# Gated linear attention feeding an expert layer: attention stages placed anew between the matrix products, with a drain of TensorE between groups of outputs

## The chip, the cores and the metric

One core of a Trainium2 chip runs the whole program. The metric is the device time of one execution in microseconds (us), as the median of the runs. TensorE (PE in the profile) multiplies matrices and is fed weights by a second row of the profile (PEld); VectorE (DVE), ScalarE (ACT) and GpSimd (POOL) do the rest, and SyncE (SP) issues nearly all transfers (DMAs).

## What is computed

Two layers follow each other. The first is attention with a decaying state, for 4 batches and 8 heads of width 48, over 768 positions; its output, 3072 tokens of 384 numbers, goes through a wide layer of 2048 units with a piecewise quadratic activation:

```python
f = 1 / (1 + exp(-f_logit))
for t in range(768):
    state = f[t] * state + outer(k[t], v[t])
    y[t] = q[t] @ state
x = y.reshape(3072, 384)
h = x @ w_in
g = where(h >= 1, h, where(h <= -1, 0, (h + 1) ** 2 / 4))
out = g @ w_out
```

## The kernel before, in words

**Tiles.** The 768 positions are cut into 6 tiles of 128 (index i). With 4 batches a tile is 512 tokens. The expert layer works tile by tile, in 16 *units* of 128 hidden columns each, so there are 96 units, numbered u = 16 i + j. `unit_1(u)` multiplies the tile with its piece of w_in (9 matrix products of 128x128 by 128x512 on line 265, 3 row blocks times 3 terms, since each fp32 number is split into a high and a low part), and then ACT and DVE form the activation: `act_1` and `act_2` on ACT (lines 268 and 271), `act_3` on DVE (line 276), the high part on ACT (line 884) and the low part on DVE (line 279). `unit_2(u)` multiplies that with the piece of w_out (9 products on line 286). TensorE gets them in the order unit_1(u), then what attention has at u, then unit_2(u-1).

**Weights.** Each of the 32 weight pieces comes in as 64-bit floats, and is turned into a high and a low part before the first tile's units need it: ACT line 362, DVE line 364, a cast on ACT or DVE (line 367), DVE line 368. This happens once, during units 0 to 15.

**Attention.** Heads are taken in pairs; n counts pairs of heads, 4 to a tile (n = 4 i + p), and stages work on n and n+1 together. The *gates* of a tile (function `gate`, 3 per tile) are an exponential and a logarithm on ACT, a running sum on DVE (line 498), two more exponentials, and two products on DVE that scale the keys and queries in place (lines 503 and 504). The fourth pair's rows are spread over the three tiles' spare rows and are gathered by small transfers (`move`, line 295). TensorE's part of attention has four stages:

- *turns*: transposes the keys (line 635; from the third tile on DVE does it, line 650);
- *scores*: keys times queries, 64 small products (line 616), masked by DVE (line 622);
- *parts*: keys times values, 64 small products (line 754), summed into the state by DVE (lines 775 and 777); *states* is its simpler form for the first tile (line 733);
- *outputs*: 32 products that mask one diagonal half (called `begin`, line 683), 64 products with the state (line 705, called `before`), and 32 products for the other half (line 683 again), all added up in two PSUM banks; ACT and DVE then round the result (lines 655 and 656) and small transfers (line 295) put it in place for the expert layer.

**Order.** The order on TensorE is written out: tables `TURNS` and `VISITS` say for each pair n at which unit each of its stages stands, and `AFTER` does so for the first tile. A stretch of small attention products stands between two runs of large ones. `begin` runs in the same stretch as `parts`, one unit or more before the rest of `outputs`. The order on ACT, DVE, SP and POOL comes from a list scheduler, `Plan.order`: each operation has a cost from the table `COST`, transfers land `LANDING` + `PER_KB` per KB after their issue, and of what is ready the one that is due first goes first. What comes out is a fixed order in which each engine waits for its operands. Where the planner sees TensorE idle for over 500 ns, it puts in filler products (function `warm`, line 331).

```python
TURNS = {4: 4, 5: 5, 6: 9, 7: 9, 8: 19, ...}
VISITS = {4: (5, 6, 7), 6: (10, 12, 13), 8: (21, 22, 25), 10: (25, 26, 28), ...}
AFTER = {0: (("turn", 0), ("turn", 1)), 1: (("states", 0),), 2: (("turn", 2), ("turn", 3)), 3: (("states", 2),)}
```

In `VISITS` the three numbers of a pair are the units of its scores, of its `begin` with `parts`, and of its outputs. Where two pairs name one unit, both stages stand in one stretch; that is so at seven units already (25, 28, 37, 40, 47, 61 and 70: outputs of one pair, then scores of the next).

Of the kernel before, what the change touches and what calls it, by code (L numbers as in the profile page):

```python
# [23 lines left out]
C = 128  # L24
# [24 lines left out]
SMALL_PRODUCTS = ("gates", "scores", "heads", "own", "tile", "both", "begin", "before", "part", "states", "parts", "half", "turn")  # L49

HOP, LANDING, PER_KB, NEAR, ADDING, PATIENCE, FLAG_BY = 200, 2200, 3.0, 3500, 1500, 0, 60000
COST = dict(gates=870, log=500, mm=227, scores=1100, heads=950, own=1200, tile=680, both=1090, begin=480, before=930, part=560, states=850, parts=830, turn=350, first=110, last=95,
            rows=316, scan=1140, dve=602, small=200, half=490, sums=467, gate=600, act=575, bits=520, join=465, part_hi=440, cast_384=330, cast=400, round=485, copy=520, turned=412, sig=538, decay=226,
# [3 lines left out]
TURNS = {4: 4, 5: 5, 6: 9, 7: 9, 8: 19, 9: 19, 10: 25, 11: 25, 12: 28, 13: 28, 14: 37, 15: 37, 16: 40, 17: 40, 18: 47, 19: 47, 20: 61, 21: 61, 22: 70, 23: 70}  # L57
VISITS = {4: (5, 6, 7), 6: (10, 12, 13), 8: (21, 22, 25), 10: (25, 26, 28), 12: (28, 32, 37), 14: (37, 39, 40), 16: (40, 46, 47), 18: (47, 60, 61), 20: (61, 69, 70), 22: (70, 75, 77)}
# [3 lines left out]
AFTER = {0: (("turn", 0), ("turn", 1)), 1: (("states", 0),), 2: (("turn", 2), ("turn", 3)), 3: (("states", 2),)}  # L62
# [11 lines left out]
class Plan:  # L74
# [40 lines left out]
    def order(self):  # L115
        index = {o: n for n, o in enumerate(self.ops)}
        for o in reversed(self.ops):
            tail = o.cost + (LANDING + PER_KB * o.kb + (ADDING if o.engine == "POOL" else 0) if o.kb else o.near)
            o.late = min((u.late - (HOP if u.engine != o.engine or len(o.choices) + len(u.choices) > 2 else 0) for u in o.users), default=0) - tail - o.late_by
# [13 lines left out]
        while done < len(self.ops):  # L133
# [33 lines left out]
            if o.kb:  # L167
                wire = max(wire, end) + PER_KB * o.kb
                end = wire + LANDING + (ADDING if o.engine == "POOL" else 0)
            else:  # L170
                end += o.near
# [11 lines left out]
def gla_moe(ctx: ExitStack, tc: tile.TileContext, ff, ld, kd, kqd, f0, vv, vl, wd, maskd, identd, gates, values, headsd, out):  # L183
# [20 lines left out]
    sd = const.tile([128, NP * B * D + 2 * B * D + 16], F32, name="sd")  # L204
    state, ds = sd[:R, 0:NP * B * D].rearrange("r (g e) -> r g e", e=D), sd[:R, NP * B * D:]
# [4 lines left out]
    later = y3[:, 0, 0:2 * B * D].bitcast(F32)  # L210
# [18 lines left out]
    half, one, up, down, top_of = (const.tile([128, 1], F32, name=a) for a in ("half", "one", "up", "down", "top_of"))  # L229
# [77 lines left out]
    def fresh(t):  # L307
        nc.gpsimd.memset(t, 0.0)

# [7 lines left out]
    set_ds = add("POOL", 200, lambda: fresh(ds[:, 2 * B * D:]))  # L317
# [85 lines left out]
    def bank(k=None):  # L403

        if k is None:
            k = turn["n"] % 3
            turn["n"] += 1
        return k, (pa[k] if k < 3 else (po + ph)[k - 3].rearrange("p (b c) -> p b c", b=B)), banks[k]
# [7 lines left out]
    def old(n, *names, of=att):  # L416

        return [] if n < 0 else [of[n].get(k) for k in names]
# [20 lines left out]
    def first_loads(n):  # L439

        c, a = att[n], LOGS[n]
        if n == NP - 1:
            ready["mask"] = add("ACT", "issue", lambda: nc.scalar.dma_start(mask_z, maskd[:, 0:C + 1]), kb=64)
# [7 lines left out]
        c["l"] = sca("log", lambda: nc.scalar.activation(spread(a), spread(a), AF.Ln, bias=one), e, set_consts)  # L451
# [31 lines left out]
    def gate(m):  # L483
# [13 lines left out]
        o = sca("log", lambda: nc.scalar.activation(ft, ft, AF.Ln, bias=one), o, set_consts)  # L497
# [17 lines left out]
    def elementwise(n):  # L515
# [34 lines left out]

        def decayed():
# [3 lines left out]
        c["db"].append(sca(B * COST["decay"], decayed, d, state_of[i - 1, p // 2], old(n - 2, "y", "se"), set_ds))  # L555

# [39 lines left out]
    def borrowed(k):  # L596

        return [(6, ph[(k + 1) % 2].rearrange("p (b c) -> p b c", b=B), [gs[k - 1]["3"]]), bank(2)]

    def freed(k, held, *by):  # L600

        lent[k + 1] = by[0]
        banks[held[1][0]] = [by[1]]

    def scores_of_two(n, k):

        c, d = att[n], att[n + 1]
        held = borrowed(k)

        def emit():  # L610
            for e in range(2):
                p = (n + e) % NP
                for m in range(B):
                    for k, h in TILES:
                        (a, z), half = HEADS[h], slice(T * k, T * k + T)
                        nc.tensor.matmul(by_block(held[h][1])[half, e * B + m], key(p, m)[a:z, half],  # L616
                                         query(p, m)[a:z, T * (1 - k):][:, :T], start=True, stop=True)
# [10 lines left out]
    def transpose_tensor(n, at=None):  # L628
        i, p = pairs[n]
        c = att[n]  # L630
        b, ps, held = bank(at)
# [6 lines left out]
        c["kn"] = [plan.either(dict(ACT="turned", DVE="turned"), lambda copy: copy(kn[n % 2][:, :, :R], ps[:, :, :R]), c["tr"], old(n - 2, "st") or att[1]["y"])]  # L638
        banks[b] = c["kn"]
# [34 lines left out]
    def attended(n, other):  # L674
# [3 lines left out]
        def emit():  # L678
            for m in range(B):
                for e, k in TILES:  # L680
# [3 lines left out]
                                     masked(n)[h][half, e * B + m], start=other and m == 0, stop=not other and m == B - 1)  # L684
# [3 lines left out]
    def begin(n):  # L688

        c, d = att[n], att[n + 1]  # L690
        c["to_y"] = held = [bank(0), bank(1)]
        c["yb"] = add("PE", "begin", attended(n, True), c["am"], c["lv"], [b[2] for b in held])

    def outputs(n):
# [3 lines left out]
        held = c["to_y"]  # L698

        def emit():  # L700
            for k, before in ((1, later), (0, ds)):
# [445 lines left out]
```

## Time and profile before

| | |
|---|---|
| median of 3 runs | 470.0 us (469.55 to 470.15) |
| span of the profiled execution, first to last instruction | 467.3 us |
| so outside the span (470.0 - 467.3) | 2.7 us |
| granted TensorE clock, mean | 0.998 |
| busy: PE, PEld, DVE, ACT, POOL | 460.3, 376.4, 346.5, 299.5, 22.7 us |
| transfers | 54.36 MB, mean 116 GB/s |

The page gives no own time of the profiled execution beside its span; the span stands for it, and what lies outside the span is taken as the same before and after. A busy PE is not PE at its peak: matrix products overlap in the array, so what counts is the time from the start of one group to the start of the next, not the durations.

### The profile page before, as it was taken

What the parts mean: (1) busy time and instruction counts of PE and PEld (TensorE: products, weight loads), DVE (VectorE), ACT (ScalarE), POOL (GpSimd) and SP (SyncE); (2) the same over time, 40 slices, a digit from 0 to 9 for tenths busy, and PEclk for the clock granted to TensorE, in tenths of its full rate; (3) what the DMA queues carried; (4) which work ended last, traced back from release to release, by engine and by line L of the source; (5) the groups of instructions that cost most, each with busy time, mean ns of one, the idle gap of its engine ahead of it and who ended that gap; (6) DMA issues with size and microseconds to landing.
All of it is one profiled execution on the core that took longest, in us unless ns stands there. A gap on an engine that the chain in (4) does not pass through costs nothing.

```text
span 467.3 us, 10979 instructions
## 1 busy us (share of the span) xinstructions
PE 460.3 (99%) x4502; PEld 376.4 (81%) x4502; DVE 346.5 (74%) x689; ACT 299.5 (64%) x551; POOL 22.7 (5%) x75
## 2 busy tenths in 40 slices
PE   8999999999999999999999999999999999999996
PEld 5887888888888788888888888888888888888884
DVE  3989998789999989989878788566766755533332
ACT  7798998999456766578475546654545454644443
POOL 2202010000000200000020001000000000000000
PEclk9999999999999999999999999999999999999999
DMA  8887686453023423053336223244322124300001
GB/s 282 297 264 246 201 264 198 150 162 111 1 69 126 114 69 102 2 193 110 74 85 211 110 67 91 68 129 128 127 81 70 67 85 120 101 3 0 1 0 71
DMA packets 21861, 54.36 MB, mean 116 GB/s; under 512 B 3568, under 2 KB 4464, under 8 KB 21808
## 3 DMA queue, kind: packets, MB, share of 16 engines
q1 hardware_dynamic: 21664, 53.57, 36.4%
q8 instruction: 36, 0.59, 0.5%
q14 instruction: 17, 0.14, 0.1%
q10 hardware_dynamic: 144, 0.07, 0.1%
HBM read 44.96 MB, written 4.72 MB: 106 GB/s over the span
## 4 chain that ended last, share of the span: by engine, by line
PE 95%; DVE 1%; ACT 1%; DMA 1%; issue 0%; SPq 0%; DVEq 0%; ACTq 0%
PE po L286 42%; PE ph L265 41%; PE pa L683 2%; PE pa L705 2%; PE ph L616 1%; DMA kq<-in_k 1%; PE po L567 1%; PE pa L754 1%; PE pa L801 1%; PE pa L635 1%; PE ph L855 0%; PE pa L460 0%; DVE act L276 0%; PE pa L616 0%; DVE kn L650 0%
## 5 line engine op out<-in xcount | busy, mean ns | idle before, releaser
L265 PE MATMUL ph<-x,w_hi 128*128 128x512 f32 x570 | 146.5, 389 | 0.0
L268 ACT ACTIVATE act<-ph,half 128x512 f32<-128x512 f32 x96 | 65.9, 687 | 93.5 <-PE ph L265 93.3
L265 PEld LDWEIGHTS ph<-x,w_hi 128*128 128x128 f32 x570 | 106.8, 188 | 22.6 <-ACT w_hi L367 0.4
L276 DVE SCALAR_TENSOR_TENSOR act<-ph,act 128x512 f32<-128x512 f32 x96 | 66.2, 690 | 63.6 <-ACT act L271 62.5
L884 ACT CAST ghi<-act 128x512 fp32r<-128x512 f32 x96 | 59.5, 620 | 51.1 <-DVE act L276 50.6
L286 PE MATMUL po<-ghi,w_hi 128*128 128x512 f32 x288 | 86.2, 401 | 1.1 <-ACT ghi L884 1.1
L286 PE MATMUL po<-ghi,w_lo 128*128 128x512 f32 x288 | 83.2, 390 | 0.0
L286 PE MATMUL po<-glo,w_hi 128*128 128x512 f32 x288 | 82.9, 389 | 0.0
L279 DVE TENSOR_TENSOR glo<-act,ghi 128x512 fp32r<-128x512 f32 x96 | 66.2, 689 | 21.5 <-ACT ghi L884 20.0
L265 PE MATMUL ph<-x,w_lo 128*128 128x512 f32 x285 | 81.7, 389 | 0.0
L650 DVE STREAM_TRANSPOSE kn<-kq 32x128 f32<-32x128 f32 x224 | 67.7, 302 | 3.6
L286 PEld LDWEIGHTS po<-ghi,w_lo 128*128 128x128 f32 x288 | 54.1, 188 | 11.6
L286 PEld LDWEIGHTS po<-glo,w_hi 128*128 128x128 f32 x288 | 54.1, 188 | 11.5
L271 ACT ACTIVATE act<-act 128x512 f32<-128x512 f32 x96 | 60.7, 632 | 2.9
L265 PEld LDWEIGHTS ph<-x,w_lo 128*128 128x128 f32 x285 | 53.5, 188 | 11.1
L286 PEld LDWEIGHTS po<-ghi,w_hi 128*128 128x128 f32 x288 | 52.0, 188 | 12.0 <-issue 0.9
L378 DVE TENSOR_REDUCE ok<-raw 128x1 f32<-128x384 f32 x64 | 33.2, 545 | 1.6 <-DMA raw<-in_w 1.6
L362 ACT ACTIVATE bits<-raw,top_of 128x384 uint32<-128x384 fp8e4 x32 | 20.0, 643 | 0.8 <-DMA raw<-in_w 0.8
L553 ACT ACTIVATE sd<-sd,kq 112x48 f32<-112x48 f32 x80 | 19.2, 325 | 0.0
L368 DVE TENSOR_TENSOR w_lo<-bits,w_hi 128x384 fp32r<-128x384 f32 x32 | 17.6, 554 | 2.0 <-ACT w_hi L367 1.7
L498 DVE TENSOR_TENSOR_SCAN w<-rec,f 128x512 f32<-128x512 f32 x15 | 18.3, 1220 | 0.9 <-ACT f L497 0.8
L502 POOL COPY end<-w 128x4 f32<-128x4 f32 x15 | 4.7, 316 | 261.1 <-ACT w L501 261.1
(135 smaller groups left out, 382.6 us busy)
## 6 DMA issues: line engine op xcount, KB each, us to landing
raw<-in_w SPq DMA_DIRECT2D x32, 384.0 KB, 3.0
raw<-in_w SPq DMA_DIRECT2D x32, 383.6 KB, 3.6
kq<-in_kq SPq DMA_DIRECT2D x15, 512.0 KB, 4.8
v<-in_v SPq DMA_DIRECT2D x12, 384.0 KB, 4.6
out_y<-raw SPq DMA_DIRECT2D x18, 256.0 KB, 2.7
f<-in_f SPq DMA_DIRECT2D x15, 256.5 KB, 2.9
kq<-in_k SPq DMA_DIRECT2D x4, 512.0 KB, 6.5
kq<-kq SPq DMA_DIRECT2D x30, 64.2 KB, 2.7
```

The source lines that it names most:

```text
L265: nc.tensor.matmul(ps, w_in(w_hi if high else w_lo, j, kt), xt[:, kt, t], start=(n == 0), stop=(n == 8))
L268: nc.scalar.activation(a, ps, AF.Relu, bias=half, scale=0.5)
L271: nc.scalar.activation(a, a, AF.Square)
L276: nc.vector.scalar_tensor_tensor(out=a, in0=ps, scalar=1.0, in1=a, op0=ALU.max, op1=ALU.min)
L279: nc.vector.tensor_tensor(out=lo, in0=a, in1=hi.bitcast(F32), op=ALU.subtract)
L286: nc.tensor.matmul(po[e], w_out(part, j, e), g, start=(j == 0 and n == 0), stop=(j == NJ - 1 and n == 2))
L362: m = sca("bits", lambda: nc.scalar.activation(t, top, AF.Abs, bias=top_of, scale=2.0 ** 30), loaded, made[k - 4] if k >= 4 else None, set ...
L378: seen.append(vec("join", lambda z=z, op=op: nc.vector.tensor_reduce(out=ok[:, 1 + NG + z + c:2 + NG + z + c], in_=words_of(raw[2])[1].bit ...
L498: s1 = vec("scan", lambda: nc.vector.tensor_tensor_scan(out=wide(w), data0=wide(rec), data1=ft[:, N:0:-1], initial=0.0, op0=ALU.mult, op1= ...
L553: nc.scalar.activation(ds[:, at + b * D:at + (b + 1) * D], state[:, p * B + b], AF.Copy, scale=pf[:R, b:b + 1])
L650: nc.vector.transpose(kn[n % 2][to:to + 32, ::-1, r:r + 32], src[:, :, u:u + 32])
L884: o = g["hi"] = sca("copy", lambda: nc.scalar.copy(hi, a), o, unit_out.get(u - 2))
```

## The change

It does five things. (1) Stages are placed anew by one table: 26 stretches where there were 29, some with two stages of different pairs. (2) `outputs` need no longer be begun in an earlier stretch: for the pairs 8, 12, 16, 18 and 22 all three groups run behind one another. Where a group of line 683 follows products of another kind into the same banks, `nc.tensor.drain()` stands between; pairs with an early `begin` (4, 6, 10, 14 and 20) drain ahead of the state's products. That is one drain for each of the 10 outputs. (3) Buffers: `later` gets two tiles of its own (it shared one with `y3`), the decayed state `ds` is doubled, and waits on the freeing of them go. (4) The planner's costs and transfer times are other numbers. (5) Five constants share one tile, and one clearing of `ds` goes. The number of attention products is the same.

```diff
-HOP, LANDING, PER_KB, NEAR, ADDING, PATIENCE, FLAG_BY = 200, 2200, 3.0, 3500, 1500, 0, 60000
-COST = dict(..., log=500, ..., both=1090, begin=480, before=930, part=560, states=850, parts=830, turn=350, first=110, last=95, ...)
+HOP, LANDING, PER_KB, EARLY, NEAR, MOVED, ADDING, PATIENCE, FLAG_BY = 200, 1700, 2.8, 600, 700, 115, 1500, 0, 60000
+COST = dict(..., log=520, ln=620, ..., both=930, before=930, part=460, behind=600, states=850, parts=720, half=370, turn=350, first=250, last=140, ...)
...
-TURNS = {4: 4, 5: 5, 6: 9, 7: 9, 8: 19, 9: 19, 10: 25, 11: 25, 12: 28, 13: 28, 14: 37, 15: 37, 16: 40, 17: 40, 18: 47, 19: 47, 20: 61, 21: 61, 22: 70, 23: 70}
-VISITS = {4: (5, 6, 7), 6: (10, 12, 13), 8: (21, 22, 25), 10: (25, 26, 28), 12: (28, 32, 37), 14: (37, 39, 40), 16: (40, 46, 47), 18: (47, 60, 61), 20: (61, 69, 70), 22: (70, 75, 77)}
+VISITS = ((0, (("turns", 0),)), (1, (("states", 0), ("turns", 2),)), (2, (("states", 2), ("scores", 4),)), (3, (("begin", 4), ("turns", 4),)),
+          (5, (("parts", 4),)), (6, (("outputs", 4),)), (7, (("scores", 6), ("turns", 6),)), (9, (("begin", 6), ("parts", 6),)), (10, (("outputs", 6),)),
+          (22, (("parts", 8), ("scores", 8),)), (24, (("outputs", 8), ("scores", 10),)), (28, (("begin", 10), ("parts", 10),)), (29, (("outputs", 10),)),
+          (33, (("parts", 12), ("scores", 12),)), (37, (("outputs", 12), ("scores", 14),)), (42, (("begin", 14), ("parts", 14),)),
+          (46, (("outputs", 14), ("parts", 16),)), (47, (("scores", 16),)), (49, (("outputs", 16),)), (53, (("parts", 18), ("scores", 18),)),
+          (56, (("outputs", 18),)), (64, (("scores", 20),)), (66, (("parts", 20),)), (69, (("begin", 20), ("scores", 22),)),
+          (75, (("outputs", 20), ("parts", 22),)), (76, (("outputs", 22),)))
...
-AFTER = {0: (("turn", 0), ("turn", 1)), 1: (("states", 0),), 2: (("turn", 2), ("turn", 3)), 3: (("states", 2),)}
...
     def dma(dst, src, kb, *deps):
-        return add("SP", "issue", lambda: nc.sync.dma_start(dst, src), *deps, kb=kb)
+        return add("SP", "issue", lambda: nc.sync.dma_start(dst, src), *deps, kb=kb, near=0 if "f0" in ready else EARLY)
     def move(dst, src, *deps):
-        return add("SP", "near", lambda: nc.sync.dma_start(dst, src), *deps, near=NEAR)
+        return add("SP", "near", lambda: nc.sync.dma_start(dst, src), *deps, kb=MOVED, near=NEAR)
...
-    def attended(n, other):
+    def attended(n, other, first):
...
         def emit():
+            if other and not first:
+                nc.tensor.drain()
             for m in range(B):
...
-    def begin(n):
+    def begin(n, other=True):
...
-        c["yb"] = add("PE", "begin", attended(n, True), c["am"], c["lv"], [b[2] for b in held])
+        c["ys"] = add("PE", "part", attended(n, other, True), c["am"], c["lv"], [b[2] for b in held])
+        c["other"] = other
...
     def outputs(n):
...
+        if "to_y" not in c:
+            begin(n, False)
+        held, begun = c["to_y"], c["other"]
         def emit():
-            for k, before in ((1, later), (0, ds)):
+            if begun:
+                nc.tensor.drain()
+            for k, before in ((1, later_of[n // 2 % 2]), (0, ds_of[n // 2 % 2])):
...
-        c["ys"] = add("PE", "before", emit, c["db"], d["db"], c["later"], c["yb"])
-        y = c["y"] = d["y"] = add("PE", "part", attended(n, False), c["ys"])
+        o = add("PE", "before", emit, c["db"], d["db"], c["later"], c["ys"])
+        y = c["y"] = d["y"] = add("PE", "part" if begun else "behind", attended(n, not begun, False), o)
```

## Rows read from the trace of the kernel before

**Rows 1.** The page, part 1: busy us, share of the span, instructions of each engine

```profile
PE 460.3 (99%) x4502; PEld 376.4 (81%) x4502; DVE 346.5 (74%) x689; ACT 299.5 (64%) x551; POOL 22.7 (5%) x75
```

**Rows 2.** The page, part 4: the chain that ended last, share by engine

```profile
PE 95%; DVE 1%; ACT 1%; DMA 1%; issue 0%; SPq 0%; DVEq 0%; ACTq 0%
```

**Rows 3.** Timeline of PE, units 13 and 14: start us, us to the last end, line, count

```profile
85.73 1.52 PE L265 MATMUL ph<-x,w_hi 128*128 128x512 f32 x6
...
87.86 0.67 PE L705 MATMUL pa<-kq,y 48*48 48x64 f32 x32
88.34 0.63 PE L705 MATMUL pa<-kq,sd 48*48 48x64 f32 x32
88.79 0.63 PE L683 MATMUL pa<-am,v 64*48 64x64 f32 x32
89.35 0.96 PE L286 MATMUL po<-ghi,w_hi 128*128 128x512 f32 x3
...
91.53 1.52 PE L265 MATMUL ph<-x,w_hi 128*128 128x512 f32 x6
...
93.57 0.84 PE L286 MATMUL po<-ghi,w_hi 128*128 128x512 f32 x3
...
95.61 1.52 PE L265 MATMUL ph<-x,w_hi 128*128 128x512 f32 x6
```

**Rows 4.** Timeline of PE around the filler products ahead of unit 5

```profile
43.50 0.60 PE L331 MATMUL po<-zeros 128*128 128x512 bf16 x2
44.04 1.66 PE L265 MATMUL ph<-x,w_hi 128*128 128x512 f32 x6
```

**Rows 5.** Timeline of PE at unit 28, last small product and next large ones

```profile
160.21 0.22 PE L616 MATMUL pa<-kq 48*64 48x64 f32 x1
161.48 0.85 PE L286 MATMUL po<-ghi,w_hi 128*128 128x512 f32 x3 [1.05 <-ACT ghi L884]
```

**Rows 6.** Timeline of ACT at unit 28; page, part 3: code packets, MB, share

```profile
157.17 0.62 ACT L884 CAST ghi<-act 128x512 fp32r<-128x512 f32 x1 [0.76 <-DVE act L276]
...
q8 instruction: 36, 0.59, 0.5%
```

**Rows 7.** Timeline of PE, units 2 and 3: the turns and the second states

```profile
30.94 0.93 PE L635 MATMUL pa<-ident,kq 112*128 112x112 f32 x8
...
35.94 0.93 PE L733 MATMUL pa<-v,kn 128*48 128x48 f32 x32
```

**Rows 8.** Windows view, 22.9 to 46.7 us: length, PE, PEld, DVE, ACT, POOL busy, clock, DMA share, GB/s

```profile
22.90:46.70 23.80, 23.80 (x173) 18.86 (x171) 22.03 (x39) 21.46 (x40) 2.88 (x6) 1.00 0.79 251
```

**Rows 9.** Groups of DVE by line, 28.8 to 36 us: count, busy us, mean ns

```profile
L368 DVE TENSOR_TENSOR w_lo<-bits,w_hi 128x384 fp32r<-128x384 f32 x3 | 1.7, 556 | 0.1
L364 DVE SCALAR_TENSOR_TENSOR bits<-raw,bits 128x384 uint32<-128x384 uint32 x3 | 1.6, 549 | 0.0
L276 DVE SCALAR_TENSOR_TENSOR act<-ph,act 128x512 f32<-128x512 f32 x2 | 1.4, 687 | 0.1
L279 DVE TENSOR_TENSOR glo<-act,ghi 128x512 fp32r<-128x512 f32 x2 | 1.4, 685 | 0.0
L638 DVE COPY kn<-pa 128x448 f32<-128x448 f32 x2 | 1.2, 622 | 0.1
L498 DVE TENSOR_TENSOR_SCAN w<-rec,f 128x512 f32<-128x512 f32 x1 | 1.2, 1220 | 0.0
L367 DVE CAST w_hi<-bits 128x384 fp32r<-128x384 f32 x2 | 0.7, 360 | 0.1
```

**Rows 10.** Timeline of DVE: the last product of the gates that scores 4 waits for

```profile
45.27 0.69 DVE L503 TENSOR_TENSOR kq<-kq,w 128x512 f32<-128x512 f32 x1
```

**Rows 11.** Groups of PE and PEld by line and shape: count, busy us, mean ns

```profile
L683 PE MATMUL pa<-am,v 64*48 64x64 f32 x640 | 12.9, 218 | 0.1
L683 PEld LDWEIGHTS pa<-am,v 64*48 64x48 f32 x640 | 10.5, 120 | 3.7 <-issue 2.1 <-DVE am L622 0.9 <-DVE glo L279 0.7
```

**Rows 12.** The page, part 6, and its like for 58 to 68 us: moves of keys, us to landing

```profile
kq<-kq SPq DMA_DIRECT2D x30, 64.2 KB, 2.7
...
kq<-kq SPq DMA_DIRECT2D x2, 64.2 KB, 4.9
```

More of the change, by code (lines that the diff above doesn't have):

```diff
@@ L46 @@
 NG = (NP + (NI - 1) * NT) * B
-SMALL_PRODUCTS = ("gates", "scores", "heads", "own", "tile", "both", "begin", "before", "part", "states", "parts", "half", "turn")
-HOP, LANDING, PER_KB, NEAR, ADDING, PATIENCE, FLAG_BY = 200, 2200, 3.0, 3500, 1500, 0, 60000
-COST = dict(gates=870, log=500, mm=227, scores=1100, heads=950, own=1200, tile=680, both=1090, begin=480, before=930, part=560, states=850, parts=830, turn=350, first=110, last=95,
-            rows=316, scan=1140, dve=602, small=200, half=490, sums=467, gate=600, act=575, bits=520, join=465, part_hi=440, cast_384=330, cast=400, round=485, copy=520, turned=412, sig=538, decay=226,
+SMALL_PRODUCTS = ("gates", "scores", "heads", "own", "tile", "both", "before", "part", "behind", "states", "parts", "half", "turn")
@@ new lines @@
+HOP, LANDING, PER_KB, EARLY, NEAR, MOVED, ADDING, PATIENCE, FLAG_BY = 200, 1700, 2.8, 600, 700, 115, 1500, 0, 60000
+COST = dict(gates=870, log=520, ln=620, mm=227, scores=1100, heads=950, own=1200, tile=680, both=930, before=930, part=460, behind=600, states=850, parts=720, half=370, turn=350, first=250, last=140,
+            rows=316, scan=1140, dve=602, small=310, sums=467, gate=600, act=585, bits=535, join=465, part_hi=420, cast_384=330, cast=400, round=485, copy=530, turned=412, sig=538, decay=226,
@@ L169, in order @@
                 end = wire + LANDING + (ADDING if o.engine == "POOL" else 0)
-            else:
-                end += o.near
+            end += o.near
             o.end = end
@@ L416, in old @@
     def old(n, *names, of=att):
-        return [] if n < 0 else [of[n].get(k) for k in names]
+        return [] if n < 0 else [of[n][k] if n >= NP and k in ("y", "st", "se", "db") else of[n].get(k) for k in names]
     LOGS = [t[:, 0:N] for t in (f[0], f[1], act_f[1], act_f[0])]
@@ L442, in first_loads @@
         if n == NP - 1:
-            ready["mask"] = add("ACT", "issue", lambda: nc.scalar.dma_start(mask_z, maskd[:, 0:C + 1]), kb=64)
+            ready["mask"] = add("ACT", "issue", lambda: nc.scalar.dma_start(mask_z, maskd[:, 0:C + 1]), kb=64, near=EARLY)
             ready["sel"] = dma(ident, identd, 64)
@@ L637, in transpose_tensor @@
         c["tr"] = add("PE", "turn", emit, c["kq"], held, ready["ident"])
-        c["kn"] = [plan.either(dict(ACT="turned", DVE="turned"), lambda copy: copy(kn[n % 2][:, :, :R], ps[:, :, :R]), c["tr"], old(n - 2, "st") or att[1]["y"])]
-        banks[b] = c["kn"]
+        c["kn"] = [plan.either(dict(ACT="turned", DVE="gate"), lambda copy: copy(kn[n % 2][:, :, :R], ps[:, :, :R]), c["tr"], old(n - 2, "st") or att[1]["y"])]
+        if b == 6:
+            lent[k + 1] = c["kn"][0]
+        else:
+            banks[b] = c["kn"]
     def transpose_rows(n):
@@ L718, in outputs, with states @@
                         for t in range(NT) for r, z in ((48, 0), (112, 64))]
-    def states(n):
-        b, ps, held = bank()
+    def states(n, place):
+        b, ps, held = place
         ps = wide(ps)
@@ L948, in gla_moe @@
     ready["minus"] = add("POOL", 1500, negative, ready["ident"])
-    work = dict(gates=first_gates, mask=masks, scores=scores, last=last_heads, heads=lambda t: half_tile(t, True), tile=lambda t: half_tile(t, False), rest=rest, unit=unit_0,
-                turn=lambda n: transpose_tensor(n, {0: 1, 1: 5}.get(n)), states=lambda n: states(n))
+    work = dict(gates=first_gates, mask=masks, scores=scores, last=last_heads, heads=lambda t: half_tile(t, True), tile=lambda t: half_tile(t, False), rest=rest, unit=unit_0,)
     for kind, n in START:
```

113 lines of the change are left out of this document (64 added, 49 removed).

## The prediction

> **What bounds the kernel now.** I read the page's busy times first, then the chain that ended last, then the timeline of TensorE. PE is busy 460.3 of 467.3 us and the chain is 95% PE [rows 1, 2]: the reader is to see that next to nothing waits ahead of TensorE, so the time is the sum of what TensorE does, one group behind another. A change can win by shortening its list, or by removing one of the few places where it stands still; it loses wherever TensorE comes to stand still anew.
>
> The timeline shows the price of a stretch of small products. In plain running a unit's nine large products take 2.04 us from start to start (91.53 to 93.57, and 93.57 to 95.61) [rows 3]. With a stretch between, unit_1 takes 85.73 to 87.86 = 2.13 us, 0.09 more; the unit_2 behind it 89.35 to 91.53 = 2.18 us, 0.14 more; and the last 32 small products hold the place 0.56 us (88.79 to 89.35), where the 32 ahead of them took 0.45 (88.34 to 88.79), 0.11 more [rows 3]. So entering and leaving costs 0.09 + 0.11 + 0.14 = 0.34 us, whatever stands in the stretch.
>
> TensorE stands still, or does filler, in two places worth naming. Ahead of unit 5 two filler products hold it 43.50 to 44.04 = 0.54 us [rows 4]. At unit 28 the large products begin 1.05 us late [rows 5]. The row names ACT's copy of ghi, but the copy that this unit needs ended at 157.17 + 0.62 = 157.79 [rows 6], long before. TensorE's code is a candidate: 4502 products and 4502 weight loads [rows 1] came in 36 packets [rows 6], some 250 instructions each, and this stretch holds 160 products, so 320 instructions, in about 2.3 us. That is a guess; the price of 1.05 us is a row.
>
> The third thing to see is DVE early on. From 22.9 to 46.7 us it is busy 22.03 of 23.80 us, ACT 21.46, and the transfers 0.79 of their time [rows 8]: besides TensorE, DVE has almost no room while it prepares the weights.
>
> **The change part by part**, in us against the span of 467.3. The median is 470.0, and the 2.7 us between are taken as unchanged.
>
> *Fewer stretches.* 29 become 26; the three that go all lie in units 0 to 13 (12 become 9). Gain 3 x 0.34 = 1.02. Later on there are 17 both before and after. The products in them are as many as before.
>
> *Filler.* The place ahead of unit 5 has other neighbours and other planned costs; I count the 0.54 as gained, and what the planner's gap stood for (weights late on DVE) goes into the early wait below.
>
> *Unit 28.* Its stretch is taken apart (outputs 10 now at 29, scores 12 at 33). Gain 1.05. Against it, stretches of two stages with 192 products now stand at units 24 and 37 (all three groups of outputs, then scores) and one with 160 at unit 46. Of the seven stretches with 160 before, one stalled; if it is code that came late, longer ones stall more often. Between no stall and one at each (0 to 3.2) I take a loss of 0.5, near the one in seven seen, with more weight on the longer ones.
>
> *Drains.* Ten. The trace has none. Below, a drain costs nothing (it only waits, so a gain is excluded). Above, it costs the last small product to its end and a weight load that cannot run ahead, 0.218 + 0.120 [rows 11], less the step of 0.03 that would be there anyway: 0.3 each, 3.0 in all. The nearest row is the end of a stretch, where the next products also wait for the array to empty: 0.11 [rows 3]. I take 0.15 for the five between small groups and 0.05 for the five at the head of a stretch, where the wait after the large products (0.09) is paid already: 5 x 0.15 + 5 x 0.05 = 1.0. (The planner's own numbers in the diff, 600 for the group behind a drain and 460 without one, say 0.14.)
>
> [...]
>
> *The early wait.* This is the part that can eat the rest. Scores 4 moves from unit 5 to unit 2, and needs the gates of two tiles' rows. Before, the last of their products ended at 45.27 + 0.69 = 45.96 [rows 10]. In the new order TensorE comes to scores 4 where the turns stood at 30.94, plus the turns (moved up) and states 2, some 0.7 each since ends overlap [rows 7]: about 32.3. TensorE works in order, so everything behind scores 4 waits with it. Can DVE make it? By 36.0 it had done none of the gates. Two of them are 2 x (1.22 + 0.69 + 0.69) = 5.2 [rows 9, 10]. What it can put off is the weights and activations of later units in 28.8 to 36: 1.7 + 1.6 + 1.4 + 0.7 (the later of two L276) + 0.7 = 6.1 [rows 9]. So 36.0 - 6.1 + 5.2 = 35.1; if all 1.8 idle [rows 8] is filled, 33.3; if two key copies of 0.62 go to ACT, 32.1. Bounds on the wait: 0 to 2.8. I take 0.7, nearer the low end, because ACT has 23.80 - 21.46 = 2.3 free [rows 8] and takes copies and casts. The weights put off come due from unit 3 on; that backlog is of the same size, and TensorE has by then been held, so I add nothing for it, but up to 1 to the upper end.
>
> *The second early wait.* Scores 6 moves from unit 10 to 7 and needs rows that are moved by transfers behind the third gate. Such moves landed 4.9 us after issue at 58 to 68 us, against 2.7 over the run [rows 12], because large loads were ahead; the planner now reckons 2.7 after the issue cost (700 + 1700 + 115 x 2.8 = 2722 ns), less than before. Between 0 and 1.5; I take 0.4. Outputs 14 two units ahead of the tile that needs them (46 for 48, before 40) has the same kind of chain; it has over 8 us for two roundings and six moves, so 0.
>
> *Kinds of product side by side.* States beside scores, begin or scores beside turns change the shape of the products inside a stretch, three times: at the entry price of 0.09, about 0.2 (0 to 0.5).
>
> *Buffers.* `later` and `ds` doubled take waits off DVE and ACT. TensorE waited for neither in the trace, so nothing. What else the planner reorders on SP, POOL, ACT and DVE is covered by TensorE after the first tile, as there is no wait of PE in its place.
>
> Sum: -1.02 - 0.54 - 1.05 + 0.5 + 1.0 + 0.7 + 0.4 + 0.2 = +0.2. I forecast a wash: 467.3 + 0.2 in the span, 470.2 us as a median, **no change** within 0.2% (0.94 us, about what a measurement of this kernel can tell from none).
>
> **The rivals.** *Faster: the plan comes true.* The scheduler finds DVE's room, the early waits are 0, no stretch stalls on code: -2.61 + 1.0 + 0.2 = -1.4, so 468.6; with drains at 0.03 each, 467.9. For it: the bounds reach 32.1 against 32.3, and TensorE waits in only a few places under the old plan, so such plans do come true here. Against it: DVE busy 93% of 22.9 to 46.7 us.
>
> *Slower: DVE becomes the bound at unit 2.* Scores 4 starts at 35.1 and the weights put off hold TensorE another 1.0 at units 4 and 5: 2.8 + 1.0 in place of 0.7 makes the sum 0.2 + 3.1 = 3.3, so 473.3; without the second hold it is 472.3. It decides when scores 4 starts later than about 33.8. For it: in-order issue and a DVE without room; against it: ACT's free 2.3 us.
>
> *Slower: a drain costs all of the pipeline*, 0.3 each: 3.0 in place of 1.0, so 472.2. [...] *It does not do what it says*: seven stretches shared two stages already, and if the new table only trades neighbours, what is left is the drains; that lies within the wash.
>
> **How the numbers follow.** Wash 0.36 (469.06 to 470.94), plan comes true 0.34, DVE bound at unit 2 0.22, dear drains 0.08. So faster 0.34, same 0.36, slower 0.30. Range: leaving out a tenth on either side, from the best sum with cheap drains (467.9) to the DVE case without its second hold (472.3): 467.8 to 472.3.
>
> **What would show it.** Right: 26 stretches, each with 0.34 over plain running; scores 4 starting 0.5 to 1 us late after the product ahead of it, waiting for DVE line 503 or 504; no filler ahead of unit 5; a drain visible as a step of about 0.15 between the last product of line 705 and the next of line 683. Wrong: scores 4 without a wait (then faster), or one above 2 us (then slower); steps of 0.3 at drains; gaps of 1 us inside or behind the stretches of units 24 and 37; or a first unit that starts elsewhere than now, since I count nothing ahead of 22.9 us.

## The result, and the profile after

| | before | after |
|---|---|---|
| median, us (lowest to highest, runs) | 469.96 (469.55 to 470.15, 4) | 474.86 (473.97 to 475.81, 4) |
| span of the profiled execution | 467.3 | 473.9 |

The ratio is 1.0104, 95% interval [1.0087, 1.0121]: **slower by 4.9 us**, above the range (467.8 to 472.3). The profiled execution took 475.81 us, about 1 more than the median.

The page after: busy times, the instruction packets, the chain of waits, the group of ACT's first step on the raw weights, and the loads of raw weights with their median us to landing.

```profile
PE 462.8 (98%) x4500; PEld 376.8 (80%) x4500; DVE 346.3 (73%) x689; ACT 297.5 (63%) x551; POOL 21.9 (5%) x74
...
q8 instruction: 36, 0.59, 0.5%
...
PE 83%; DMA 6%; ACT 4%; DVE 3%; issue 2%; SPq 0%; DVEq 0%; ACTq 0%
...
L363 ACT ACTIVATE bits<-raw,biases 128x384 uint32<-128x384 fp8e4 x32 | 20.1, 641 | 6.3 <-DMA raw<-in_w 6.3
...
raw<-in_w SPq DMA_DIRECT2D x32, 383.6 KB, 4.4
```

The same two lines on the page of before:

```profile
L362 ACT ACTIVATE bits<-raw,top_of 128x384 uint32<-128x384 fp8e4 x32 | 20.0, 643 | 0.8 <-DMA raw<-in_w 0.8
...
raw<-in_w SPq DMA_DIRECT2D x32, 383.6 KB, 3.6
```

TensorE has as much to do as before [rows 1], but the chain is 83% PE where it was 95% [rows 2], and what came in is transfers. ACT waits 6.3 us for raw weights where it waited 0.8. What TensorE itself waited for, all of its list of waits after (us in total, times, longest):

```profile
PE pa L696 <- DMA v<-in_v: 1.2, 1, 1.2
PE ph L332 <- DVE zeros L310: 1.1, 1, 1.1
PE ph L624 <- issue: 0.8, 1, 0.8
PE po L291 <- ACT ghi L905: 0.6, 1, 0.6
PE ph L876 <- ACT x L666: 0.4, 1, 0.4
PE po L571 <- DVE kq L471: 0.3, 1, 0.3
```

Five places explain most. **The first unit** starts at 21.61 us instead of 20.74. The timelines of ACT and then PE after (start us, us):

```profile
18.84 0.64 ACT L363 ACTIVATE bits<-raw,biases 128x384 uint32<-128x384 fp8e4 x1 [1.13 <-DMA raw<-in_w]
19.39 0.50 ACT L368 CAST w_hi<-bits 128x384 fp32r<-128x384 f32 x1
20.45 0.63 ACT L498 ACTIVATE f<-f 128x513 f32<-128x513 f32 x1 [0.57 <-DMA f<-in_f]
20.99 0.57 ACT L666 CAST x<-pa 128x512 fp32r<-128x512 f32 x1
...
5.16 1.67 PE L462 MATMUL pa<-mask,act 128*112 128x128 f32 x8
...
21.61 0.50 PE L876 MATMUL ph<-x,w_lo 128*128 128x512 f32 x1 [0.40 <-ACT x L666]
```

ACT takes its list in order: at unit 10, below, it starts at 85.41 on products that had ended at 83.56. Its new list has a step on raw and one on f ahead of the cast of x that unit 0 needs; both wait for loads (f was issued at 14.08 and landed at 20.43). Part of the 0.87 us may lie elsewhere: the first eight products behind the filler took 1.67 us, in the profile of before 1.13 (a4, below, looks at the two apart). Inside unit 0 the casts of x come late once more: 2.63 us to the first turn instead of 2.18.

**Unit 3.** The masked half of outputs 4 waits for a load of v. PE, start us, us:

```profile
38.77 0.84 PE L270 MATMUL ph<-x,w_lo 128*128 128x512 f32 x3
40.78 0.67 PE L696 MATMUL pa<-am,v 64*48 64x64 f32 x32 [1.17 <-DMA v<-in_v]
```

The load was issued at 35.53 and landed at 40.65, 5.1 us later; the planner's new times give 1.7 + 2.8 x 0.384 = 2.8. It had to wait for the states of unit 2 to read the buffer, but their last product ended at 34.03. What held it after that is SP's own list, which SP takes in order:

```profile
32.90 1.90 SPq L300 DMA_DIRECT2D kq<-kq  x3
34.85 0.62 SPq L297 DMA_DIRECT2D raw<-in_w  x1
35.53 0.42 SPq L297 DMA_DIRECT2D v<-in_v  x1
```

Three moves and a raw load stand ahead of v. Issued at 34.03 and as long under way, v would have landed at 39.2 (an estimate), ahead of 39.54, where TensorE came to it.

**Unit 10.** ACT, then PE:

```profile
84.86 0.64 ACT L363 ACTIVATE bits<-raw,biases 128x384 uint32<-128x384 fp8e4 x1 [1.73 <-DMA raw<-in_w]
...
87.59 0.61 ACT L905 CAST ghi<-act 128x512 fp32r<-128x512 f32 x1
...
88.26 0.96 PE L291 MATMUL po<-ghi,w_hi 128*128 128x512 f32 x3 [0.61 <-ACT ghi L905]
```

The load landed 6.0 us after issue. Behind ACT's wait stand the activation and ghi, and PE comes 0.78 us late.

**Drains.** One between small products, and one behind a large product:

```profile
140.43 0.63 PE L726 MATMUL pa<-kq,sd 48*48 48x64 f32 x32
141.20 0.67 PE L696 MATMUL pa<-am,v 64*48 64x64 f32 x32
...
54.90 0.84 PE L270 MATMUL ph<-x,w_lo 128*128 128x512 f32 x3
55.85 0.66 PE L726 MATMUL pa<-kq,later 48*48 48x64 f32 x32
```

From 140.43 to 141.20 is 0.77 us, where the like took 0.45 in before [rows 3]: 0.32 more. At the head, the last large product holds the place 0.50 us, 0.32 without a drain: 0.18 more. Five of each: 1.59 + 0.89 = 2.48 us.

**Unit 37**, inside a stretch of outputs and scores:

```profile
204.27 0.22 PE L624 MATMUL pa<-kq 48*64 48x64 f32 x1
205.29 0.27 PE L624 MATMUL ph<-kq 48*64 48x64 f32 x1 [0.80 <-issue]
```

"issue" says that no wait is known. The gap of before at unit 28 [rows 5] is gone.

By starts of PE: +0.87 and +0.45 (unit 0), +1.24 (unit 3, less the usual entry), +0.78 (unit 10), +2.48 (drains), +1.02 (unit 37), +1.20 (the end, where the last output landed 3.22 us after issue, before 2.13), less 0.54 (filler), 1.12 (unit 28) and 1.02 (three stretches, at the prediction's price): 5.4 of 6.6 us. The rest is in small steps; 0.4 of it are four places where small products of different kinds meet (0.139 to 0.149 us from start to start, elsewhere 0.03).

### The profile page after: what moved, and what is told of

The parts are those of the page before. It is cut to its first block, busy times and chain, and to the rows that moved or that the text cites. A ratio compares the mean times of both kernels' runs of the same rounds, so it can differ in the third digit from the quotient of the medians.

```text
span 473.9 us, 10960 instructions
## 1 busy us (share of the span) xinstructions
PE 462.8 (98%) x4500; PEld 376.8 (80%) x4500; DVE 346.3 (73%) x689; ACT 297.5 (63%) x551; POOL 21.9 (5%) x74
## 4 chain that ended last, share of the span: by engine, by line
PE 83%; DMA 6%; ACT 4%; DVE 3%; issue 2%; SPq 0%; DVEq 0%; ACTq 0%
PE po L291 38%; PE ph L270 36%; DMA raw<-in_w 3%; PE pa L696 2%; PE pa L726 2%; DMA f<-in_f 1%; DMA v<-in_v 1%; PE ph L624 1%; PE pa L624 1%; ACT bits L363 1%; PE pa L462 1%; ACT sd L557 1%; PE pa L775 1%; DMA kq<-in_kq 1%; DMA raw<-in_l 1%
## 5 line engine op out<-in xcount | busy, mean ns | idle before, releaser
L273 ACT ACTIVATE act<-ph,biases 128x512 f32<-128x512 f32 x96 | 65.9, 686 | 103.0 <-PE ph L270 102.2
L284 DVE TENSOR_TENSOR glo<-act,ghi 128x512 fp32r<-128x512 f32 x96 | 66.2, 689 | 22.3 <-ACT ghi L905 20.4
L363 ACT ACTIVATE bits<-raw,biases 128x384 uint32<-128x384 fp8e4 x32 | 20.1, 641 | 6.3 <-DMA raw<-in_w 6.3
L365 DVE SCALAR_TENSOR_TENSOR bits<-raw,bits 128x384 uint32<-128x384 uint32 x32 | 17.2, 551 | 1.8 <-ACT bits L363 1.8
```

Of the source, the lines that this page charges most:

```text
L273: nc.scalar.activation(a, ps, AF.Relu, bias=half, scale=0.5)
L284: nc.vector.tensor_tensor(out=lo, in0=a, in1=hi.bitcast(F32), op=ALU.subtract)
L363: m = sca("bits", lambda: nc.scalar.activation(t, top, AF.Abs, bias=top_of, scale=2.0 ** 30), loaded, made[k - 4] if k >= 4 else None, set ...
```

## The experiments

Theory: the drains were mis-sized, the planner's new transfer times cost some 2 us that were put at nothing, and the gaps of 1 us are code that comes late. Each kernel has its own runs of before, taken together with it (medians 469.92 to 470.3); "ratio" is to those, over all runs, so it can differ a little from that of the medians. Below, a *step* is the time from the start of one product to the start of the next.

**Drains alone.** a1: before, with a drain ahead of the state's products of each of the 10 outputs. a2: one behind them.

```diff
+            nc.tensor.drain()
             for k, before in ((1, later), (0, ds)):
```

> The kernel before, with a drain of TensorE at the head of each of its 10 groups of outputs, right behind the large products; places and planner as they were. If a drain there costs what the trace of after shows (0.496 us from the last large product to the first small one, against 0.318), ten cost 10 x 0.18 = 1.8 us and the median goes from 470.0 to 471.8. If the wait behind the large products pays for it, as the prediction had it (0.05 each), 470.5.

> The kernel before, with a drain between the state's products and the last 32 products of each of its 10 groups of outputs. If a drain between small groups costs what the trace of after shows (0.353 us from product to product against 0.036), ten cost 3.2 us: 473.2. By the prediction's price of 0.15 each: 471.5. By the planner's 0.14: 471.4.

a1: 472.40, ratio 1.0052 [1.0036, 1.0067]. a2: 473.29, ratio 1.0061 [1.0038, 1.0083]. PE of a2:

```profile
88.85 0.63 PE L707 MATMUL pa<-kq,sd 48*48 48x64 f32 x32
89.61 0.66 PE L685 MATMUL pa<-am,v 64*48 64x64 f32 x32
```

0.76 us for what took 0.45 in before [rows 3]; ten such steps are 3.1 us, where the medians are 3.4 apart and the ratio says 2.9. In a1 ten steps of 0.18 are 1.8 of 2.5; 0.7 more, in the profiled execution, is a wait of the turns at 68.4 us for a move. So the price depends on the place: 0.18 behind large products, 0.32 between small ones. Ten in a kernel with nothing else changed cost about 2.5 us at the heads and 2.9 to 3.4 between small products.

c2 takes the other side: the change with the planner's old times (a3, below) and without its five head drains, whose products then stand directly behind large ones, as in before.

```diff
-            if begun:
-                nc.tensor.drain()
```

> The changed kernel with the planner's old transfer times and without the five drains at the head of outputs begun early; those five groups then stand behind large products with nothing between, as the groups of outputs do in the kernel before. Theory: each of these drains cost 0.18 us, so 0.9 less than a3_old_transfers, 471.4 us (471.0 to 471.9); the step from the last large product to the first small one goes from 0.50 to 0.32. Rival (the step behind a large product has other causes, the longer list of waits there): the steps stay at 0.5 and the time at 472.3.

472.27, ratio 1.0052 [1.0034, 1.0069]; a3 had 1.0054. A miss in the time, not in the steps: the head steps fell from 0.50 to 0.32 us, 0.89 in all. In this execution a new wait for weights (0.4 us at 52.6), a step that is 0.2 too long at 253 and a gap at unit 37 of 1.1 instead of 0.9 took most of it back. The five drains between small products were not taken out; their price rests on their steps and on a2.

**The planner's transfer times.** a3: the change with the old times. b1: before with the new ones. d3 and d4: the change with the old time for moves alone, and for loads alone (177 keeps a move at 177 + 2200 + 115 x 3.0 = 2722 ns).

```diff
 # a3
-HOP, LANDING, PER_KB, EARLY, NEAR, MOVED, ... = 200, 1700, 2.8, 600, 700, 115, ...
+HOP, LANDING, PER_KB, EARLY, NEAR, MOVED, ... = 200, 2200, 3.0, 0, 3500, 0, ...
 # d3
+HOP, LANDING, PER_KB, EARLY, NEAR, MOVED, ... = 200, 1700, 2.8, 600, 3500, 0, ...
 # d4
+HOP, LANDING, PER_KB, EARLY, NEAR, MOVED, ... = 200, 2200, 3.0, 0, 177, 115, ...
```

> The kernel after, with the planner's transfer times of before (2200 + 3.0 per KB, moves 3500, nothing extra at the start); places, drains and other costs as after. Theory: transfers that land later than planned put ScalarE to waiting in order, at the start (unit 0 begins at 21.6 us instead of 20.7 and takes 0.45 longer) and at 87 us (0.8 us): all of it comes back, about 2 us, so 472.8. Rival: the start and the wait at 87 us come of the new places, which want attention's gates earlier: then less than 0.5 us comes back.

> The kernel before with one part of the change alone: the planner's transfer times (a load is planned to land after 1.7 us and 2.8 ns a KB where it was 2.2 and 3.0, a move of keys likewise, and instructions may be placed up to 0.6 us earlier). Places of the attention stages, filler and drains stay as before. Theory: loads land later than these times say (in the changed kernel the load of raw took 6.0 us from issue to landing where ACT stood behind it), ACT takes its instructions in order, and so waits for a transfer with finished work behind it. Then unit 0 starts 0.5 to 1.0 us later than the 20.74 us of before, another gap or two of 0.3 to 0.8 us stand between the stages, and the time is 471 to 472.4 us. Rival: the shorter times do harm only together with the new places (a buffer of v that comes free late); then the time is within 0.3 us of before, unit 0 starts by 20.9 us.

> The changed kernel with the planner's old time for moves of keys alone (3.5 us), its loads as changed. Theory (the loads do the harm: the three waits seen, for f and raw ahead of unit 0, for v at unit 3 and for raw at unit 10, are all for loads): as the changed kernel, 474.5 to 475.5 (the planner puts 2 filler products back, 0.54). Rival (the moves' shorter time does it): 472.4 to 473.

> The changed kernel with the planner's old time for loads alone (2.2 us and 3.0 ns a KB), its moves as changed; TensorE's order is that of a3_old_transfers. Theory (loads): 472.0 to 473.0, no wait for v at unit 3. Rival (moves): 474.5 or more.

a3: 472.36, ratio 1.0054 [1.0035, 1.0074], half of the loss back. Unit 0 starts at 20.68, the waits at units 3 and 10 are gone, and ACT's wait for raw is 1.6 instead of 6.3 us. New is a step of 0.79 us at 33.5 (0.15 in plain running), where the products behind scores 4 wait for DVE's w_hi. b1: 472.19, ratio 1.0036 [1.0022, 1.0051], so the times cost 1.7 us under the old places too, though not by the same waits. One place in b1, DVE and then PE:

```profile
260.60 1.01 DVE L377 TENSOR_REDUCE ok<-raw 128x1 f32<-128x384 f32 x2 [1.96 <-DMA raw<-in_w]
261.53 0.68 DVE L278 TENSOR_TENSOR glo<-act,ghi 128x512 fp32r<-128x512 f32 x1
...
262.26 0.96 PE L285 MATMUL po<-glo,w_hi 128*128 128x512 f32 x3 [0.32 <-DVE glo L278]
```

A check of the weights that nobody is in need of waits 1.96 us for its load, and glo, which TensorE does need, stands behind it. In b1 DVE waits 7.9 us for raw in all, before 1.6. But TensorE loses only 0.48 us here, and the largest loss is another: seven new filler products hold it for 1.6 us at 375 us, where the new plan has TensorE idle (DVE's new order has the activation late, and ghi is not there before 377.3). Unit 0 starts at 21.05, but so it does in a1 and a2 with the plan of before (21.1).

d3: 476.33, ratio 1.0121 [1.0100, 1.0141]; two filler products came back, and the wait for v is longer:

```profile
40.35 0.67 PE L696 MATMUL pa<-am,v 64*48 64x64 f32 x32 [1.63 <-DMA v<-in_v]
```

d4: 473.70, ratio 1.0074 [1.0058, 1.0090], without a wait for v, but with other waits (0.7 us at 34.0 and 0.4 at 56.3 for weights, 0.6 at 127.7 for DVE). d3 came out above its 475.5 and d4 above its 473.0, so both missed their times. They agree on the side: the loads' old time alone gives back 0.0030 of the ratio, all old times 0.0050, and the moves' old time alone nothing. What the moves add on top of the loads is open, as the intervals of d4 and a3 overlap.

a4 leaves the times and takes the early step away: `begin` of outputs 4 at unit 5 instead of 3.

```diff
-(3, (("begin", 4), ("turns", 4),)), (5, (("parts", 4),)),
+(3, (("turns", 4),)), (5, (("begin", 4), ("parts", 4),)),
```

> The kernel after, with the begin of pair 4 at unit 5 (in the stretch of its parts) instead of unit 3. Theory: at unit 3 it waits for the transfer of the values, whose place in memory the states of unit 2 free so late; that is 1.2 us of TensorE (1.56 us from product to product against 0.32), and it comes back: 473.6. Rival (the prediction's): the vector engine is the bound in these units, so TensorE waits as long for weights at units 4 to 6 instead, and less than 0.4 us comes back.

473.90, ratio 1.0077 [1.0053, 1.0101]. The wait for v is gone; two others stand behind it:

```profile
47.08 1.67 PE L270 MATMUL ph<-x,w_hi 128*128 128x512 f32 x6 [0.70 <-ACT w_hi L368]
...
57.94 0.96 PE L291 MATMUL po<-ghi,w_lo 128*128 128x512 f32 x3 [0.26 <-DVE w_lo L369]
```

By starts of PE these two are 0.87 + 0.43 = 1.3 us, as much as the wait for v was: that is the rival's mechanism, though the time is that of the theory. The profiled execution gains elsewhere: the gap at unit 10 (0.78) is not there, and that of unit 37 is 0.2 shorter. While the weights come in, a wait taken away was here replaced by the next. And unit 0 starts at 21.44 us, though the first eight products took 1.13 us as in before. The nine runs with the plan of before start it at 20.4 to 21.1 us, so ACT's order makes 0.3 us of the late start at least, and up to 0.7 against before itself.

**Code that comes late.** If the gap is code that comes late, a fixed number of instructions at a time, shifting the sequence must move the gap of unit 28. The prediction has some 250 to a packet, from products, weight loads and packets [rows 1, 6]; the 256 of the expectations is shown by no row of before, only by the counts behind b3. b2, b3, c1 and d1 are before with other filler in place of the first 9 products; c1 and d1 keep TensorE's work there the same.

```diff
-    add("PE", 3700, lambda: warm(9), set_zeros)
+    add("PE", 3700, lambda: short(24, 128), set_zeros)   # b2: 32 columns of weights, 128 through; +30
+    add("PE", 3700, lambda: short(46, 100), set_zeros)   # b3: +74
+    add("PE", 3700, lambda: full(24, 48), set_zeros)     # c1: 128 columns of weights, 4 x 48 through; +30
+    add("PE", 3700, lambda: full(35, 33), set_zeros)     # d1: 4 x 33 through; +52
```

> The kernel before with its 9 filler products ahead of the first unit given as 24 shorter ones (32 columns of weights, 128 columns through), about as long in all; nothing else differs. TensorE's sequence is 30 instructions longer from there on. Theory: the gap of 1.05 us at unit 28 is code that comes late, because one run of small products there holds the whole of one block of 256 instructions; shifted by 30 the block's two ends no longer both lie in one run anywhere, the gap is gone and nothing takes its place: 468.9 us (468.5 to 469.3), PE idle ahead of the po products of unit 28 under 0.2 us. Rival: the gap is ScalarE's ghi that comes late, as the row's releaser has it; then the gap stays at 1.0 to 1.2 us and the time at 469.9.

> The same with 46 short products in place of the 9: 74 instructions more. Theory (late code): the block's two ends now fall inside the runs of small products of units 40, 47, 61 and 70, each of which stalls 0.9 to 1.3 us about 320 instructions after it began, while that of unit 28 is gone; 472.5 to 473.5 us. Rival (ScalarE's work is late at unit 28, and code does not matter): no new gap at these four units, the gap at unit 28 stays, the time is within 0.4 us of before.

b3: 473.82, ratio 1.0083 [1.0056, 1.0109]. PE, the first instructions behind the gaps at units 40, 47, 61 and 70:

```profile
220.71 0.97 PE L286 MATMUL po<-ghi,w_hi 128*128 128x512 f32 x3 [0.98 <-ACT y L659]
...
255.20 0.86 PE L286 MATMUL po<-ghi,w_hi 128*128 128x512 f32 x3 [1.56 <-issue]
...
318.04 0.96 PE L286 MATMUL po<-ghi,w_lo 128*128 128x512 f32 x3 [0.66 <-issue]
...
359.48 0.21 PE L620 MATMUL pa<-kq 48*64 48x64 f32 x1 [1.50 <-issue]
```

All four named units stall, and unit 28 does not; the time is 0.3 above the forecast, with a wait of 1.3 us for a move at 68.4 beside the four. Three rows say "issue" and one names ACT, for one and the same thing. That is why the row of before could name ghi [rows 5].

The traces show the code itself. TensorE's instructions can be counted in order: weight loads, products and the sequencer's own, 9066 in before, over 36 packets of 16 KB (16384 bytes) some 252 to each. Behind 100 us the 18 profiled executions have 19 steps over 0.5 us. Three of them wait for DVE; at the other 16, in 13 kernels, the count ahead of the late product and its weight load is 192 or 193 above a multiple of 256 (3776 is 14 x 256 + 192 in before), and a packet of 16 KB of code ended 1.2 to 1.6 us ahead of it. The stretch of unit 28 in before (157.93 to 161.48) and a time ahead of the same stretch in d1, below (154.9 to 156.2; the stretch is 157.75 to 160.73), have these lines for code:

```profile
q8 instruction: 1, 0.02, 2.1%
...
q8 instruction: 1, 0.02, 4.6%
```

In before the packet comes inside the stretch (159.07 to 160.27), and TensorE goes on at 161.48; in d1 it is there before the stretch begins, and nothing stalls. What makes a packet come earlier or later is not shown.

b2: 470.65, ratio 1.0012 [0.9997, 1.0027], a miss. Of the gap 0.38 us is left, now inside the stretch, and three waits ahead of it and behind it (0.64 at 41.3 for w_hi, 0.3 more at 68.4, 0.28 at 325.8) took back the rest. Its filler also ended 1.1 us earlier, so c1 keeps the filler's length.

> The kernel before with its first 9 filler products given as 24 of 192 columns with the full 128 columns of weights: the same work for TensorE in all, 30 instructions more. The earlier b2_code_30 ended its filler 1.1 us sooner, and in its like b4_old_transfers_code_30 the first products after it then ran at half the pace, which may have cost what the code gave. Theory (late code at unit 28, worth 1.0 to 1.1 us): PE idle ahead of the po products of unit 28 under 0.4 us, the first 8 mask products take 1.1 to 1.7 us as before, time 468.7 to 469.2 us. Rival (what a shift gives at unit 28 is taken back by waits on transfers in the first 100 us, whatever the filler): 469.8 to 470.7 us, with new gaps ahead of 100 us that sum to 0.7 or more.

c1: 470.00, ratio 0.9998 [0.9985, 1.0011]. PE at unit 28 in c1:

```profile
160.95 0.22 PE L621 MATMUL ph<-kq 48*64 48x64 f32 x1
161.86 0.21 PE L621 MATMUL ph<-kq 48*64 48x64 f32 x1 [0.69 <-issue]
```

The gap was not gone. It stood 292 instructions into the stretch where before it stood 322 in, behind the last product, and is 0.91 us long: the gap kept its count from the start of the program (3776), and the stretch moved past it by the 30 that were added. Both theory and rival of that run were wrong about it; 30 was too little.

> The kernel before with its first 9 filler products given as 35 of 132 columns: the same work for TensorE, 52 instructions more. With 30 more the gap at unit 28 stood 292 instructions into its stretch, where without it stood 322 in. Theory (late code: a block of 256 instructions that is entered and left inside one stretch stalls, unless TensorE's fetch entered it while still behind large products): with 52 more the block is entered 15 instructions into the stretch, while the large products ahead still run, and the gap goes: no step over 0.4 us at unit 28, 468.8 to 469.3 us. Rival (a stretch of 160 products at unit 28 stalls wherever the code stands): a gap of 0.8 to 1.1 us some 270 instructions in, 469.8 to 470.3.

d1: 469.24, ratio 0.9981 [0.9968, 0.9995]. At unit 28:

```profile
160.59 0.22 PE L621 MATMUL pa<-kq 48*64 48x64 f32 x1
...
160.73 0.96 PE L286 MATMUL po<-ghi,w_hi 128*128 128x512 f32 x3
```

0.14 us, as at any other stretch, and no new gap behind unit 0. This kernel, before with the filler cut differently, is **faster than before**, by 0.9 us.

b4 is a3 with the filler of b2, against the gap at unit 37.

> The changed kernel with the planner's old transfer times (as the earlier run a3_old_transfers, 472.36 us) and the 24 short filler products (30 instructions more). Theory: the stall of 0.94 us inside the run of small products of unit 37 is late code and goes; 471.4 us (471.0 to 471.8), and what is left above the kernel before is the drains (0.18 and 0.32 us each, 2.5 in all) less the saved stretches and filler. Rival (the stall is something of the stage at unit 37 itself): it stays at 0.8 to 1.1 us and the time at 472.4.

473.14, ratio 1.0059 [1.0040, 1.0077]. The gap is gone, but unit 0 starts at 22.61 us. The shorter filler ended 1.27 us before the next products, and PE then did this:

```profile
5.07 2.05 PE L466 MATMUL pa<-mask,act 128*112 128x128 f32 x8 [1.27 <-ACT act L457]
6.91 1.91 PE L466 MATMUL pa<-mask,f 128*112 128x128 f32 x8
```

These products take 1.13 and 1.13 us in before, and unit 0 starts 1.9 us later than in a3. But b2 has the same filler:

```profile
5.06 1.13 PE L464 MATMUL pa<-mask,act 128*112 128x128 f32 x8 [1.25 <-ACT act L455]
```

So the idle time alone does not make them slow, and what does is open. b4 cannot tell the price of the gap. c3 can.

**The filler ahead of unit 5, and all together.** c4 is c1, and d2 is d1 with 37 products of 4 x 31, both without the two products at 43.50 [rows 4]:

```diff
-                elif o.start > 20000 and gap > 500:
+                elif o.start > 20000 and gap > 50000:
```

> The kernel before with the 24 products of 192 columns and without the 2 filler products ahead of unit 5: two things that the change brought, alone. Theory: 0.54 us for the filler beside 1.05 for the code, 468.4 us (468.0 to 468.9), faster than both kernels. Rival: the filler covers a wait for weights; then TensorE waits 0.3 to 0.6 us ahead of unit 5 instead and the time is as that of c1_code_30_full.

> The same shift (37 products of 124 columns) without the 2 filler products ahead of unit 5, which gave 0.5 us in c4_code_30_no_filler (469.53). Theory: 468.5 us (468.0 to 469.0), below both kernels by more than a measurement is uncertain. Rival: as c4, 469.4 or more.

c4: 469.53, ratio 0.9992 [0.9980, 1.0004]. d2: 470.07, ratio 0.9985 [0.9968, 1.0002]. PE of c4, which is like d2 here:

```profile
42.48 0.85 PE L286 MATMUL po<-glo,w_hi 128*128 128x512 f32 x3
...
43.70 1.67 PE L265 MATMUL ph<-x,w_hi 128*128 128x512 f32 x6 [0.37 <-ACT w_hi L372]
```

The rival holds for the place: the step there is 0.54 us too long without the filler, as long as the filler. It covered a wait for weights. The times fit it, but not closely: seven of d2's twelve runs lie at 470.0 to 470.9 and five, the profiled one among them, at 468.0 to 469.1, and why is open.

c3 is c2 with the filler of c1: old times, no head drains, and the code shifted.

> The same with the 24 products of 192 columns (30 instructions more). Theory: the stall of 0.94 us at unit 37 goes, 470.5 us (470.0 to 471.0): what is left of the change is then the saved stretches and filler (-1.6), unit 28 (-1.1) against the five drains between small products (+1.6), the early waits of about 1 and so a wash with the kernel before, as predicted. Rival (the change has a further price that I have not found): 471.3 or more.

470.76, ratio 1.0020 [1.0008, 1.0033]: no gap at unit 37, and 4.0 of the 4.9 us are back. What is left (0.9 by the ratio) is the balance of what the change still costs, the five drains between small products (1.6 us) and waits in the first 100 us, and what it saves. The planner's new costs and the buffers were not tried alone; what they do is in that balance. This execution has a wait of 0.9 us at unit 10 for a load again, so such waits don't hang on the planned times alone.

## Why the prediction was wrong

Its sum was +0.2; the medians say +4.9, the profiled executions +6.6.

- *Failed:* "I count nothing ahead of 22.9 us", and "what else the planner reorders on SP, POOL, ACT and DVE is covered by TensorE after the first tile". The trace has 1.3 us at unit 0 and 0.8 at unit 10, with ACT in order behind a load, and a3 puts the new transfer times at 2.4 us (b1 at 1.7 under the old places, most of it at another place). The prediction read them in the diff and used them for moves only, though giving the moves alone their old time gained nothing (d3).
- *Failed:* of `begin` moved to unit 3 it counted no input but the buffers, at nothing. The load of v cost 1.24 us. The wait feared at scores 4 (0.7), for DVE, was at most 0.25 and that at scores 6 (0.4) is not there. DVE made it; what was late was a transfer, behind others in SP's list, which was not looked at. With the old times DVE is the late one after all, by 0.6 us for weights behind scores 4 (a3, c2, c3, d4), so the term was not idle, but the new times put other waits in its place.
- *Mis-sized:* drains, 1.0 against 2.48. The 0.15 between small products measured 0.32, the upper bound that was worked out from the rows (0.3); the 0.05 at the head measured 0.18, so the entry does not pay for it. The rival of 0.3 each came nearer with 3.0.
- *Mis-sized:* filler, 0.54 by the list, but c4 and d2 show that its place then waits as long. The prediction put that wait into another term instead of naming it as the cover of this one.
- *Right:* unit 28 as late code (1.05, measured 1.12), and a new stall of that kind in the longer stretches: 0.5 counted as a chance, 1.02 at unit 37, one of the three places named. That it was one is luck: not the length alone decides but where the count of 192 falls, 319 instructions into the stretch at unit 37, 283 at unit 24 and 185 at unit 46. Right too are 26 stretches. Kinds side by side gave about 0.4 instead of 0.2.

The rival "DVE becomes the bound" came nearest with 473.3, but by another road, so that is no merit of it. A wait in the first 90 us at each of three places for a load stood in no rival. Whether the end (1.2) belongs to the change is not shown: from the last product to the end of the span the profiled executions take 4.6 to 5.7 us with places of before and 4.9 to 6.8 with those of the change.

## What to carry to other kernels

Where a list scheduler orders engines that work in order, a transfer time that is planned too short is an edit to every engine's list. Here work that waits for a load was put ahead of work that TensorE needs (ACT waited 6.3 us for raw where it had waited 0.8; the new times cost 2.4 us by a3), so compare planned landings with the issues and landings of the trace. A drain between small products (0.32 us) cost as much as entering and leaving a stretch (0.34), so merging stages at that price saves nothing. A gap of about 1 us in or behind a long stretch of small products, with no plausible releaser, as at units 28 (1.12) and 37 (1.02), may be code; shift the sequence by some tens of instructions and see whether the gap stays at its count from the start of the program while the stretch moves past it.

## What the runs showed of the hardware that was not expected

- TensorE stalled (steps of 0.8 to 1.8 us) where the count of its instructions passed 192 above a multiple of 256 late in a run of small products, and each time a packet of 16 KB of code had ended 1.2 to 1.6 us before. The bound was sharp: with that count 296 instructions or more into the stretch there was a gap in each of 15 cases, with 289 or fewer in none. Between, c1 (292) had one of 0.9 us, b2 (292) one of 0.38 and c3 (293) none.
- Eight equal products took 1.13, 1.67 and 2.05 us at the start of three executions (before, after, b4). The views give the granted clock as 1.00 in that stretch each time, but the trace's first record of it (1.00) begins at 4.55 us in before, ahead of these products, and at 6.31 in after, amid them: there they start 0.21 us apart up to that time and 0.11 from then on, and in before 0.11 apart (the first step of each, 0.35 and 0.20, aside). Ahead of the 2.05, TensorE had idled 1.27 us behind a shorter filler, but b2 took 1.13 behind the same filler and 1.25 us of idling. That the clock comes late in after is one reading; what slows them in b4 is open.
- Loads of 384 KB landed 5.1 to 6.5 us after issue at the places where others waited for them in after, against medians over a run of 3.0 to 4.4 for the raw weights (before and after).
